# A 1x1 depthwise-separable convolution on one core: early loads dealt to two queues in another way, x's first chunk held by a semaphore, two filler matmul pairs and a warm-up copy dropped

## The chip, the core and the metric

The kernel runs on one core of a Trainium2 chip. The metric is the device time of one execution in microseconds (us). Three runs of the kernel before gave 573.46 us at the median. A profiled execution has a time of its own, and its trace covers a span from the first to the last instruction that is a little shorter. The engines are named as in the profile: PE is TensorE (PEld its weight loads), DVE VectorE, ACT ScalarE, POOL GpSimd, SP SyncE. ACTq and SPq are the instruction streams of ACT and SP where they issue DMAs; each of the two has a DMA queue of its own (q10 for ACT and q1 for SP in the profile), and both queues use the same 16 DMA engines.

## The reference

`x` is bf16 `[1, 384, 384, 384]`, that is 147456 rows of 384 channels; `dw` is `[1, 1, 384]`, one factor a channel; `pw` is `[384, 384]`.

```python
H = W = 384; C = 384; k = 1
x  = normal(1, H, W, C) * 0.05      # bf16
dw = normal(k, k, C) * 0.05         # bf16
pw = normal(C, C) * 0.05            # bf16

out = x * dw[0, 0]                  # k = 1: no padding, one tap
return einsum('bhwc,cd->bhwd', out, pw)
```

So the result is `x @ (diag(dw) @ pw)`, one matrix product with a scaled weight.

## The kernel before

The 147456 rows are worked on in 288 supertiles of 512 rows. SP loads rows of x into SBUF (three big buffers X0 to X2, in chunks of 1, 2, 4, 5, 6 or 10 supertiles; the first four chunks hold one supertile each). DVE transposes them in 32 by 32 blocks of 32-bit words into T (lines 404 and 406), in two halves a supertile; two T buffers alternate. PE multiplies: a supertile is 12 steps of 4 matmuls that run side by side in the four row quarters of the array (line 264), with the scaled weight `w_r` as the moving operand, into one of two PSUM buffers. ACT copies PSUM to bf16 in SBUF (line 475), and SP stores it. The loop over supertiles counts semaphores; the order on each engine is the order in which the program was written.

The change lies ahead of that loop, in the first microseconds, where the weight is made:

- Four loads are issued ahead of everything else (helper `load_early`, line 118): `dw` and the three 128-row parts of `pw` (k = 0, 1, 2, tile `raw`), and x's first chunk, 384 KB (tile `X`). The other loads of x follow on SP (line 170).
- PE fills the time with matmuls on constant ones, whose results nobody reads: two passes of four in `idle_work` ahead of the section, two more behind (line 134), two pairs at line 295 and some pairs between the useful ones.
- Three tiny matmuls turn dw into a column (line 282), DVE makes selection matrices scaled by dw from it (line 435), and for each k and r = 0, 1 a pair of matmuls (line 295) puts the scaled, regrouped rows of pw's part k into PSUM. These are called units i = 2k + r below. Each increments `s_w`.
- The units are copied from PSUM to `w_r` (line 422), by the table `w_units` of (unit, from, to, engine): unit 0 by ACT, unit 1 half by ACT and half by DVE, unit 2 by DVE, units 3, 4 and 5 by ACT, each engine in this order.
- Behind its two copies, DVE makes the first three transposes of x's first chunk (line 404); it comes to them only when its copies are done.
- PE starts the loop when units 0 to 3 are in `w_r` and the first transpose is done. Unit 4 is first needed at the ninth of the twelve steps, unit 5 at the eleventh.

On ACT a small copy to a tile `warm` (line 377) stands ahead of the `w_r` copies, and an activation table load ahead of that. The copy, and a memset on DVE, also give PSUM's two buffers free at the start (`s_a`).

Of the kernel before, what the change touches and what calls it, by code (L numbers as in the profile page):

```python
# [9 lines left out]
F32 = mybir.dt.float32  # L10
# [17 lines left out]
def kernel(  # L28
# [12 lines left out]
    nc = tc.nc  # L41
    P = nc.NUM_PARTITIONS
    B, H, W, C = x.shape
    assert dw.shape[0] == 1 and dw.shape[1] == 1, "only k=1 depthwise supported"
    D = pw.shape[1]
# [4 lines left out]
    xf = x.rearrange("b h w c -> (b h w) c")  # L50
# [25 lines left out]
    pw_n = raw[:, 0 : 3 * D].rearrange("p (k d) -> p k d", d=D)  # L76
# [6 lines left out]
    warm = consts.tile([P, 2], F32, name="warm")  # L83
# [3 lines left out]
    X0_h = nc.alloc_sbuf_tensor("X0", [P, 4 * LMAX, C], BF16)  # L87
# [5 lines left out]
    PS_h = [nc.alloc_psum_tensor(f"ps{s}", [P, 4, 512], F32) for s in range(2)]  # L93
    PS = [h.ap() for h in PS_h]

    s_x = [[nc.alloc_semaphore(f"s_x{i}{k}") for k in range(max(map(len, groups[i::NR])))] for i in range(NR)]
# [5 lines left out]
    s_a = [nc.alloc_semaphore(f"s_a{i}") for i in range(2)]  # L102
# [4 lines left out]
    s_pw = [nc.alloc_semaphore(f"s_pw{k}") for k in range(3)]  # L107
# [2 lines left out]
    s_dwf = nc.alloc_semaphore("s_dwf")  # L110
    s_sel = nc.alloc_semaphore("s_sel")
    s_w = nc.alloc_semaphore("s_w")
    s_wr = [nc.alloc_semaphore(f"s_wr{e}") for e in range(2)]

    early = []

    def load_early(eng, dst, src, sem):
        ins = eng.dma_start(dst, src).then_inc(sem, 16)  # L118
        tc.no_tile_sem_insts.add(ins.ins.name)
        early.append(ins.ins.name)  # L120

    dw_e = dataclasses.replace(dw_h, donated_from="early_dw").ap()
    pw_e = [dataclasses.replace(raw_h, donated_from=f"early_pw{k}").ap()[:, D * k : D * k + D] for k in range(3)]
    load_early(nc.scalar, dw_e, dw.rearrange("a e c -> a (e c)"), s_dw)
    for k in range(3):
        load_early(nc.scalar if k == 2 else nc.sync, pw_e[k], pw[P * k : P * k + P, :], s_pw[k])
    x0 = xf[0:512, :].rearrange("(p s) c -> p (s c)", p=P)
    X0_e = dataclasses.replace(X0_h, donated_from="early_x0").ap()[:, 0:4].rearrange("p s c -> p (s c)")
    load_early(nc.sync, X0_e, x0, s_x[0][0])

    def idle_work(ps, n):
        for _ in range(n):
            for i in range(4):
                mm = nc.tensor.matmul(  # L134
                    ps[:, 2 * (i % 2) + i // 2, :D],
                    lhsT=ones[32 * i : 32 * i + 32, 0:P],
                    rhs=ones[32 * i : 32 * i + 32, :],
                    start=True,
                    stop=True,
                    tile_position=(32 * i, 0),  # L140
                )
        return mm

    mm = idle_work(dataclasses.replace(PS_h[0], donated_from="early_ps").ap(), 2)
    early.append(mm.ins.name)

    with tc.tile_critical(sync_engine=mybir.EngineType.Pool, no_gpsimd_drain=True) as section:
        in_order = mybir.DependencyInfo(mybir.DependencyClass.NoSync, mybir.DependencyReason.SCHED_ONLY)
# [65 lines left out]
        def w_after(i):  # L214
            n = [sum(u[3] == e and u[0] <= i for u in w_units) for e in range(2)]
            return [(s_wr[e], n[e]) for e in range(2)]
# [64 lines left out]
        for k in range(3):  # L281
            mm = nc.tensor.matmul(  # L282
                PS[1][:, 2 + (k > 0), D + k : D + k + 1],
                lhsT=dw_row[:, P * k : P * k + P],
                rhs=ones[0:1, 0:1],
                start=True,
                stop=True,
            )
# [3 lines left out]
        def pair(out, lhsT, rhs, cols):  # L292
            for v in range(2):
                rows = slice(64 * v, 64 * v + 64)
                mm = nc.tensor.matmul(  # L295
                    out[:, v, :cols], lhsT=lhsT[rows], rhs=rhs[rows, :cols], start=True, stop=True, tile_position=(64 * v, 0)
                )
            return mm
# [3 lines left out]
        for k in range(3):  # L302
            for r in range(2):
                sel_kr = sel_w[:, k, r].rearrange("p q w -> p (q w)")
                if r == 0:
                    nc.tensor.wait_ge(s_pw[k], 16)
                if k == 0 or r == 0:
                    nc.tensor.wait_ge(s_sw, r + 1 if k == 0 else k + 2)
                if (k, r) == (0, 1):
                    nc.tensor.wait_ge(s_dwf, 2)  # L310
                if k == 2:
                    for sem, v in w_after(r):
                        if v:
                            nc.tensor.wait_ge(sem, v)

                if k == 2:
                    pair(PS[1][:, 2 * r :], sel_kr, pw_n[:, k, :], D if r == 0 else D // 2)
                pair(PS[(k + 1) % 2][:, 2 * r :], sel_kr, pw_n[:, k, :], D).then_inc(s_w)
                if (k, r) == (0, 1):
                    pair(PS[0], sel_kr, pw_n[:, k, :], D // 2)  # L320
# [22 lines left out]
        for m in range(4):  # L343
            if m == 1:
                nc.tensor.wait_ge(s_t[1][1], NS // 2)
            for par in range(2):
                mm = nc.tensor.matmul(  # L347
                    PS[1][:, m, :D],
                    lhsT=Tk[:, P * (m + 2) : P * (m + 3), par],
                    rhs=w_k[:, par, :],  # L350
                    start=False,
                    stop=par == 1,
                )
# [18 lines left out]
        for n in range(4):  # L372
            for g in range(4):
                x_b = Xl[quads[g], n, 256:384].rearrange("p (b c) -> p b c", c=64)
                nc.gpsimd.tensor_copy(Xk[quads[n], g:8:4, :], x_b).then_inc(s_xk)  # L375
                nc.gpsimd.tensor_copy(Xk[quads[n], 8 + g : 24 : 4, :], Xl[quads[g], :, 64 * n : 64 * n + 64]).then_inc(s_xk)  # L376
        nc.scalar.copy(warm[:, 0:1], nc.const_aps.tensor(0.0, [P, 1], F32)).then_inc(s_a[0])  # L377
        nc.vector.memset(warm[:, 1:2], 0.0).then_inc(s_a[1])

        def transposes(t, j):  # L380
            g, i, off, first, L = chunks[t]
# [61 lines left out]
        ins = nc.vector.tensor_copy(dw_f[:], dw_p[:, 1, 1:3])  # L443
# [10 lines left out]
        for jj, (t, j) in enumerate(order):  # L454
            g, i, off, first, L = chunks[t]
            s = jj % 2
# [64 lines left out]
```

## Time and profile before

| what | us |
|---|---|
| median of 3 runs | 573.46 |
| lowest and highest of them | 573.25, 575.51 |
| profiled execution, its own time | 573.07 |
| span of its trace | 571.1 |
| PE busy | 566.3 |
| DVE busy | 509.8 |
| ACT busy | 418.0 |
| first matmul of the loop starts at | 5.92 |

The page shows PE busy in nearly all of the span, and a DMA share of nine tenths or more in most of its slices at a mean of 397 GB/s. The loop's matmuls (line 264) have 559.8 us of PE's 566.3. What stands ahead of the loop is best read in the timeline of the first seven microseconds, beside the chain of work that ended last, whose first pieces are the early issues on SP and x's first chunk. A row of the timeline gives the start, the length, the engine, the line, the operation and the count; a bracket behind it gives the idle time before it and what ended it.

### The profile page before, as it was taken

Reading aid. Unit: us, or ns where it says so; the run is one execution under the profiler, and the core shown is the slowest. Engines: PE = TensorE matmul, PEld = TensorE weight load, DVE = VectorE, ACT = ScalarE, POOL = GpSimd, SP = SyncE. Lnnn points to the kernel's source line nnn. Section 1 sums busy time; section 2 is a strip of 40 time slices with the busy share of each in tenths; the row PEclk is TensorE's granted clock in tenths of the full one; section 3 lists DMA queues with packets and bytes.
Section 4 is the critical chain, followed back from the end, with each engine's and each line's share of the span. In section 5 each row is a group of like instructions: output and inputs, shape, how many; then the busy total and the mean of one; then the engine's idle time right before and its main releaser. Section 6 shows DMA issues by size and latency. Waiting matters only on the chain.

```text
span 571.1 us, 29717 instructions
## 1 busy us (share of the span) xinstructions
PE 566.3 (99%) x13841; PEld 359.1 (63%) x13841; DVE 509.8 (89%) x591; ACT 418.0 (73%) x297; POOL 13.9 (2%) x41
## 2 busy tenths in 40 slices
PE   8999999999999999999999999999999999999997
PEld 5666666666666666666666666666666666666664
DVE  7899999999999999999999999999999899998996
ACT  6777777777777777777777777777777777777775
POOL 2042000000000000000000000000000000000000
PEclk9999999999999999999999999999999999999999
DMA  8999999999999999999999999999999999998777
GB/s 325 436 406 391 431 418 426 436 427 410 430 433 431 404 388 425 405 383 398 431 386 396 410 427 386 409 400 421 402 394 431 402 387 402 420 394 322 312 286 269
DMA packets 28100, 226.88 MB, mean 397 GB/s; under 512 B 1465, under 2 KB 7866, under 8 KB 24122
## 3 DMA queue, kind: packets, MB, share of 16 engines
q1 hardware_dynamic: 27012, 225.81, 97.5%
q10 hardware_dynamic: 1078, 0.98, 0.5%
q14 instruction: 9, 0.07, 0.0%
q8 instruction: 1, 0.02, 0.0%
HBM read 113.54 MB, written 113.25 MB: 397 GB/s over the span
## 4 chain that ended last, share of the span: by engine, by line
PE 98%; DMA 1%; SPq 0%; ACT 0%; DVE 0%; issue 0%
PE ps L264 98%; DMA X<-in_x_dram 1%; PE ps L347 0%; SPq L118 0%; PE ps L335 0%; ACT O L470 0%; DVE T L404 0%
## 5 line engine op out<-in xcount | busy, mean ns | idle before, releaser
L264 PE MATMUL ps<-w_r,T 32*128 32x384 bf16 x13776 | 559.8, 321 | 0.6 <-DVE T L404 0.6
L406 DVE STREAM_TRANSPOSE T<-X 128x384 uint32<-128x384 uint32 x571 | 501.2, 879 | 53.5 <-DMA X<-in_x_dram 0.8
L475 ACT CAST O<-ps 128x1536 bf16<-128x1536 f32 x286 | 411.4, 1438 | 147.1 <-PE ps L264 147.1
L264 PEld LDWEIGHTS ps<-w_r,T 32*128 32x128 bf16 x13776 | 356.2, 93 | 204.2 <-DVE T L404 1.0
L376 POOL COPY Xk<-Xl 32x256 bf16<-32x256 bf16 x16 | 6.3, 394 | 0.0
L375 POOL COPY Xk<-Xl 32x128 bf16<-32x128 bf16 x16 | 4.6, 287 | 25.7 <-DMA Xl<-in_x_dram 24.9
L370 POOL COPY raw<-w_r 32x768 bf16<-32x768 bf16 x4 | 3.3, 819 | 5.7 <-ACT w_r L422 5.5
L422 ACT CAST w_r<-ps 128x768 bf16<-128x768 f32 (+1 forms) x5 | 3.3, 741 | 0.1
L377 ACT ACT_TABLE_LOAD x1 | 1.3, 1283 | 1.9 <-issue 1.9
L295 PE MATMUL ps<-raw 64*128 64x384 bf16 (+1 forms) x18 | 2.3, 419 | 0.0
L134 PE MATMUL ps<-const-bfloat16-1.0 32*128 32x384 bf16 x16 | 1.5, 515 | 0.8 <-PEq L505 0.8
L466 DVE CAST O<-ps 128x384 bf16<-128x384 f32 x2 | 1.0, 553 | 1.4 <-PE ps L264 1.4
L295 PEld LDWEIGHTS ps<-raw 64*128 64x128 bf16 x18 | 1.1, 116 | 1.5 <-DMA raw<-in_pw_dram 1.2
L406 DVE STREAM_TRANSPOSE T<-Xl 128x384 uint32<-128x384 uint32 x2 | 1.8, 884 | 0.2
L422 DVE CAST w_r<-ps 128x384 bf16<-128x384 f32 (+1 forms) x2 | 1.4, 758 | 0.2 <-PE ps L295 0.2
L389 DVE STREAM_TRANSPOSE T<-Xk 128x384 uint32<-128x384 uint32 x2 | 1.2, 578 | 0.5 <-PE ps L264 0.4
L347 PE MATMUL ps<-raw,T 128*128 128x384 bf16 x8 | 1.5, 328 | 0.0
L470 ACT CAST O<-ps 128x384 bf16<-128x384 f32 x2 | 1.0, 478 | 0.7 <-PE ps L347 0.7
L470 DVE CAST O<-ps 128x384 bf16<-128x384 f32 x2 | 1.1, 558 | 0.1
L465 ACT CAST O<-ps 128x384 bf16<-128x384 f32 x2 | 0.9, 482 | 0.5 <-PE ps L264 0.5
L347 PEld LDWEIGHTS ps<-raw,T 128*128 128x128 bf16 x8 | 0.7, 98 | 0.7 <-issue 0.3
L435 DVE TENSOR_SCALAR raw<-sel,ps 128x128 bf16<-128x128 f32 x2 | 0.5, 287 | 0.6 <-PE ps L282 0.6
(19 smaller groups left out, 5.8 us busy)
## 6 DMA issues: line engine op xcount, KB each, us to landing
X<-in_x_dram SPq DMA_DIRECT2D x25, 3840.0 KB, 21.8
out_dram<-O SPq DMA_DIRECT2D x25, 3840.0 KB, 27.8
X<-in_x_dram SPq DMA_DIRECT2D x3, 1536.0 KB, 18.0
X<-in_x_dram SPq DMA_DIRECT2D x2, 1920.0 KB, 15.6
out_dram<-O SPq DMA_DIRECT2D x2, 1920.0 KB, 24.4
out_dram<-O SPq DMA_DIRECT2D x2, 1536.0 KB, 12.9
X<-in_x_dram SPq DMA_DIRECT2D x6, 384.0 KB, 4.9
out_dram<-O SPq DMA_DIRECT2D x3, 768.0 KB, 5.3
```

Source lines behind the costliest of these rows:

```text
L134: mm = nc.tensor.matmul(ps[:, 2 * (i % 2) + i // 2, :D], lhsT=ones[32 * i : 32 * i + 32, 0:P], rhs=ones[32 * i : 32 * i + 32, :], start=Tr ...
L264: mm = nc.tensor.matmul(PS[s][:, q, :D], lhsT=Ts[s][32 * q : 32 * q + 32, b, par::2], rhs=w_r[32 * q : 32 * q + 32, b, par, :], start=(b, ...
L295: mm = nc.tensor.matmul(out[:, v, :cols], lhsT=lhsT[rows], rhs=rhs[rows, :cols], start=True, stop=True, tile_position=(64 * v, 0))
L347: mm = nc.tensor.matmul(PS[1][:, m, :D], lhsT=Tk[:, P * (m + 2) : P * (m + 3), par], rhs=w_k[:, par, :], start=False, stop=par == 1,)
L370: nc.gpsimd.tensor_copy(w_k[quads[n]], w_r[quads[n], n]).then_inc(s_wk)
L375: nc.gpsimd.tensor_copy(Xk[quads[n], g:8:4, :], x_b).then_inc(s_xk)
L376: nc.gpsimd.tensor_copy(Xk[quads[n], 8 + g : 24 : 4, :], Xl[quads[g], :, 64 * n : 64 * n + 64]).then_inc(s_xk)
L377: nc.scalar.copy(warm[:, 0:1], nc.const_aps.tensor(0.0, [P, 1], F32)).then_inc(s_a[0])
L406: ins = nc.vector.transpose(out=Tw[:, 3 * h : 3 * h + 3], in_=Xw[:, :, j, 96 * h : 96 * h + 96].rearrange("p k (b w) -> p b k w", w=32),)
L422: o = nc.vector.tensor_copy(out, in_) if e == 0 else nc.scalar.copy(out, in_)
L470: o = (nc.scalar.copy if n % 2 else nc.vector.tensor_copy)(Ov[:, n, j, :], PS[s][:, n, :D])
L475: a = nc.scalar.copy(Ov[:, :, j, :], PS[s][:, :, :D])
```

## The change

Four edits, all ahead of the loop:

1. pw's second part (k = 1) is loaded by ACT's queue, behind dw, where SP's queue had it; pw's third part (k = 2) stays on ACT's queue and so comes behind the second.
2. x's first chunk is now the second load on SP's queue, behind pw's first part, and waits for a new semaphore `s_e`. PE increments it with the last matmul of its first filler pass.
3. The two filler pairs ahead of units 4 and 5 on PE are left out.
4. The copy to `warm` on ACT is left out; DVE sets both halves of `warm` and both semaphores by two memsets.

```diff
-        load_early(nc.scalar if k == 2 else nc.sync, pw_e[k], pw[P * k : P * k + P, :], s_pw[k])
-    x0 = xf[0:512, :].rearrange("(p s) c -> p (s c)", p=P)
-    X0_e = dataclasses.replace(X0_h, donated_from="early_x0").ap()[:, 0:4].rearrange("p s c -> p (s c)")
-    load_early(nc.sync, X0_e, x0, s_x[0][0])
+        load_early(nc.scalar if k else nc.sync, pw_e[k], pw[P * k : P * k + P, :], s_pw[k])
...
-    mm = idle_work(dataclasses.replace(PS_h[0], donated_from="early_ps").ap(), 2)
-    early.append(mm.ins.name)
+    ps_e = dataclasses.replace(PS_h[0], donated_from="early_ps").ap()
+    for i in range(2):
+        mm = idle_work(ps_e, 1)
+        if i == 0:
+            mm.then_inc(s_e)
+            tc.no_tile_sem_insts.add(mm.ins.name)
+        early.append(mm.ins.name)
+
+    x0 = xf[0:512, :].rearrange("(p s) c -> p (s c)", p=P)
+    X0_e = dataclasses.replace(X0_h, donated_from="early_x0").ap()[:, 0:4].rearrange("p s c -> p (s c)")
+    load_early(nc.sync, X0_e, x0, s_x[0][0])._wait_ge(s_e, 1)
...
-                if k == 2:
-                    pair(PS[1][:, 2 * r :], sel_kr, pw_n[:, k, :], D if r == 0 else D // 2)
                 pair(PS[(k + 1) % 2][:, 2 * r :], sel_kr, pw_n[:, k, :], D).then_inc(s_w)
...
-        nc.scalar.copy(warm[:, 0:1], nc.const_aps.tensor(0.0, [P, 1], F32)).then_inc(s_a[0])
-        nc.vector.memset(warm[:, 1:2], 0.0).then_inc(s_a[1])
+        for i in range(2):
+            nc.vector.memset(warm[:, i : i + 1], 0.0).then_inc(s_a[i])
```

Lines move by a few: 118 becomes 119, 134 becomes 133, 264 becomes 272, 295 becomes 303, 404 becomes 410, 422 becomes 428.

On SP, from the program's start, the kernel before has these rows (`raw` is pw's tile, `X` x's first buffer; the counts behind a row are equal instructions in sequence):

```order
L516 UNCONDITIONAL_BRANCH [waits barrier_Pool_Activation_PE_DVE_SP_release]
L118 DMA raw<-in_pw_dram 128x384 x2
L118 DMA X<-in_x_dram 128x1536
L516 UNCONDITIONAL_BRANCH [waits Pool_sequencer_49]
L170 DMA X<-in_x_dram 128x1536 x3
```

and the changed kernel, at the same place on SP:

```order
L522 UNCONDITIONAL_BRANCH [waits barrier_Pool_Activation_PE_DVE_SP_release]
L119 DMA raw<-in_pw_dram 128x384
L119 DMA X<-in_x_dram 128x1536 [waits s_e]
L522 UNCONDITIONAL_BRANCH [waits Pool_sequencer_49]
L178 DMA X<-in_x_dram 128x1536 x3
```

One load of pw is gone from ahead of x's first chunk, which has got a wait; all later loads of x stand behind that wait.

On ACT, from the program's start to the `w_r` copies, before:

```order
L118 DMA dw_row<-in_dw_dram 1x384
L118 DMA raw<-in_pw_dram 128x384
L516 UNCONDITIONAL_BRANCH [waits Pool_sequencer_49]
L377 ACT_TABLE_LOAD
L377 COPY warm<-const-float32-0.0 128x1
L422 CAST w_r<-ps 128x2x384 [waits s_w]
```

and changed:

```order
L119 DMA dw_row<-in_dw_dram 1x384
L119 DMA raw<-in_pw_dram 128x384 x2
L522 UNCONDITIONAL_BRANCH [waits Pool_sequencer_49]
L428 ACT_TABLE_LOAD
L428 CAST w_r<-ps 128x2x384 [waits s_w]
```

A third DMA issue stands ahead of the table load, and the copy behind it is gone; the table load still comes ahead of the first wait for `s_w`.

On PE, from unit 2 to the loop (`raw` here holds pw's parts and the scaled selection matrices), before:

```order
L295 MATMUL ps<-raw 128x384 [waits s_sw,s_pw1]
L295 MATMUL ps<-raw 128x384 x3
L295 MATMUL ps<-raw 128x384 [waits s_wr1,s_sw,s_pw2]
L295 MATMUL ps<-raw 128x384 x3
L295 MATMUL ps<-raw 128x192 [waits s_wr1,s_wr0]
L295 MATMUL ps<-raw 128x192
L295 MATMUL ps<-raw 128x384 x2
L321 UNCONDITIONAL_BRANCH
```

and changed:

```order
L303 MATMUL ps<-raw 128x384 [waits s_sw,s_pw1]
L303 MATMUL ps<-raw 128x384 x3
L303 MATMUL ps<-raw 128x384 [waits s_wr1,s_sw,s_pw2]
L303 MATMUL ps<-raw 128x384
L303 MATMUL ps<-raw 128x384 [waits s_wr1,s_wr0]
L303 MATMUL ps<-raw 128x384
L327 UNCONDITIONAL_BRANCH
```

Two filler matmuls of 384 columns and two of 192 are gone; units 4 and 5 still stand behind the wait for pw's third part, and ahead of the loop.

More of the change, by code (lines that the diff above doesn't have):

```diff
@@ L112 @@
     s_w = nc.alloc_semaphore("s_w")
+    s_e = nc.alloc_semaphore("s_e")
     s_wr = [nc.alloc_semaphore(f"s_wr{e}") for e in range(2)]
@@ L120, in load_early @@
         early.append(ins.ins.name)
+        return ins
     dw_e = dataclasses.replace(dw_h, donated_from="early_dw").ap()
```

## The prediction

> **What bounds the kernel now.** I read the page first (busy times and groups), then the stretch from 20 to 560 us, then the chain of work that ended last, then the first seven microseconds row by row. From the page, the groups of instructions (count, busy us, mean ns, idle time before them), and then the row of the stretch 20 to 560 us:
>
> ```profile
> L264 PE MATMUL ps<-w_r,T 32*128 32x384 bf16 x13776 | 559.8, 321 | 0.6 <-DVE T L404 0.6
> L406 DVE STREAM_TRANSPOSE T<-X 128x384 uint32<-128x384 uint32 x571 | 501.2, 879 | 53.5 <-DMA X<-in_x_dram 0.8
> ```
> ```profile
> core 0: us, PE busy (x) PEld busy (x) DVE busy (x) ACT busy (x) POOL busy (x), PEclk, DMA share, GB/s
> 20.00:560.00 540.00, 540.00 (x13300) 343.76 (x13296) 487.90 (x555) 398.31 (x278) 10.09 (x32) 1.00 0.99 402
> ```
>
> PE is busy for all 540 of 540 us, and the loop's matmuls lost only 0.6 us in all, to DVE's first transposes at line 404. No edit touches the loop, so its 559.8 us stay. What can change is when it starts. The chain of work (start, us, what), over the first 20 us:
>
> ```profile
> 0.80 0.39 SPq L118
> 1.20 0.06 issue
> 1.26 0.41 SPq L118
> 1.67 0.05 issue
> 1.72 3.82 DMA X<-in_x_dram
> 5.53 0.02 issue
> 5.55 0.32 DVE T L404
> 5.88 0.05 issue
> 5.92 14.14 PE ps L264 x341
> ```
>
> Two pw issues, then x's first chunk issued at 1.72 and landed 3.82 later, at 5.53-5.54; 0.32 for the first transpose, and the loop starts at 5.92. The weights run beside it (timeline of ACT and DVE):
>
> ```profile
> 1.93 1.28 ACT L377 ACT_TABLE_LOAD   x1 [1.93 <-issue]
> 3.22 0.19 ACT L377 COPY warm<-const-float32-0.0 128x1 f32<-128x1 f32 x1
> 3.48 3.32 ACT L422 CAST w_r<-ps 128x768 bf16<-128x768 f32 x5
> ...
> 3.80 1.44 DVE L422 CAST w_r<-ps 128x384 bf16<-128x384 f32 x2 [0.22 <-PE ps L295]
> 5.55 0.70 DVE L404 STREAM_TRANSPOSE T<-X 128x128 uint32<-128x128 uint32 x3 [0.32 <-DMA X<-in_x_dram]
> ```
>
> DVE has finished its weight copies at 3.80 + 1.44 = 5.24 and waits 0.32 us for x. So the x path has no more than about 0.3 us to give before DVE's own weight copies hold the loop. That is the ceiling of the gain: 0.05% of the time.
>
> **The change, part by part.** 0.5% of this kernel is 2.9 us, about what its measurement can tell from no change; every term below is far smaller.
>
> *x's first chunk.* The hold is PE's first filler pass, and the issue behind pw's first part is bounded by this row and by the next issue slot on SP:
>
> ```profile
> 0.84 0.51 PE L134 MATMUL ps<-const-bfloat16-1.0 32*128 32x384 bf16 x4 [0.84 <-PEq L505]
> ```
>
> The pass ends at 1.35; with the 0.05 us that the chain shows from a signal to its taker, SP issues at 1.40, against 1.72. Without the hold it could have gone at 1.26, where the second pw load stood, so the hold costs 0.14 of the 0.46 that the freed slot gives. Bounds of the gain in issue time: 0.2 (a slower wake-up) to 0.46. With the same 3.82 us to land: 5.22. Behind the waiting instruction on SP stand only the other loads of x, which then also go 0.3 us sooner.
>
> *pw's second part.* It moves from SP at 1.26 to ACT behind dw, at 1.37, where pw's third part stood. How long such loads take to land (KB each, median us):
>
> ```profile
> raw<-in_pw_dram SPq DMA_DIRECT2D x2, 96.0 KB, 2.1
> raw<-in_pw_dram ACTq DMA_DIRECT2D x1, 96.0 KB, 2.9
> ```
>
> Two ends: 1.37 + 2.1 = 3.47 and 1.37 + 2.9 = 4.27; before it was 1.26 + 2.1 = 3.4. I take 4.27, because the ACT row is the same queue, the same issue time and a load that ran beside x's first chunk, and x now comes earlier still. The stretches 3.20 to 4.00 show the collision (all DMAs: last column GB/s), and the packets of the ACT queue q10 in 2.6 to 2.8, its first ones of pw, and then in 3.2 to 3.4, 3.6 to 3.8 and 3.8 to 4.0 (none in between):
>
> ```profile
> 3.20:3.40 0.20, 0.20 (x4) 0.15 (x2) 0.20 (x2) 0.19 (x2) 0.00 (x0) 1.00 2.25 211
> 3.40:3.60 0.20, 0.20 (x6) 0.05 (x2) 0.18 (x1) 0.13 (x2) 0.00 (x0) 1.00 0.17 15
> 3.60:3.80 0.20, 0.20 (x6) 0.19 (x4) 0.00 (x0) 0.20 (x1) 0.00 (x0) 1.00 0.34 69
> 3.80:4.00 0.20, 0.20 (x4) 0.07 (x2) 0.20 (x1) 0.20 (x1) 0.00 (x0) 1.00 0.63 253
> ```
> ```profile
> q10 hardware_dynamic: 17, 0.01, 24.2%
> ...
> q10 hardware_dynamic: 11, 0.01, 9.0%
> ...
> q10 hardware_dynamic: 2, 0.00, 2.2%
> ...
> q10 hardware_dynamic: 6, 0.00, 6.8%
> ```
>
> When x's first packets start, nearly nothing moves for some 0.4 us (15 and 69 GB/s), and ACT's last 8 packets of pw come only afterwards. In the kernel before only these stragglers of the third part were caught. Now x's packets should start about 0.3 us sooner, at the time when ACT's queue starts its first pw load, so the second part as a whole meets that standstill.
>
> What follows from 4.27: PE takes unit 2 at 4.32. The matmul rows of 3.9 to 4.2 and DVE's copy of unit 2:
>
> ```profile
> L295 PE MATMUL ps<-raw 64*128 64x384 bf16 x4 | 0.8, 524 | 0.0
> ...
> 4.28 0.96 DVE L422 CAST w_r<-ps 128x768 bf16<-128x768 f32 x1
> ```
>
> 4.32 + 0.52 + 0.03 = 4.87; DVE's copy ends at 4.87 + 0.96 = 5.83 instead of 5.24, and x, landed at 5.22, now waits for DVE. First transpose and hand-over, 0.32 + 0.05: the loop starts at 6.20, 0.28 later than before. By the other end, 3.47, PE is ready for unit 2 no sooner than before, DVE ends at 5.24, and the loop starts at 5.24 + 0.37 = 5.61, 0.31 sooner. The two meet where pw's second part lands at 5.55 - 0.96 - 0.55 - 0.05 = 3.99.
>
> [...]
>
> *pw's third part.* Issued at 1.37 + 0.37 + 0.05 = 1.79. Ends: 1.79 + 2.9 = 4.69, or 1.79 + 3.82 = 5.61 if it fares as x's chunk does. Units 4 and 5 stand ahead of the loop on PE, two pairs of 0.16 us at the loop's pace or 0.32 at the slow one (rows under D). At 4.69 they are through by 5.4, far ahead of 6.20; at 5.61 by about 6.0 to 6.3, still nearly covered by DVE. I take 0; the high end adds 0.2 if the loop otherwise would start early.
>
> *ACT.* The rows of the issue that there is now one more of, and of unit 3's copy:
>
> ```profile
> 1.37 0.37 ACTq L118 DMA_DIRECT2D raw<-in_pw_dram  x1
> ...
> 4.60 0.80 ACT L422 CAST w_r<-ps 128x768 bf16<-128x768 f32 x1
> ```
>
> One issue more, 0.37 + 0.03, moves the table load from 1.93 to 2.33; it ends at 3.61, and the first weight copy starts at 3.62 instead of 3.48. The dropped copy of 0.19 gives part of it back already. Unit 3, needed at the loop's start, would by that end at 5.40 + 0.14 = 5.54, just ahead of the earliest start worked out above. ACT's five copies were back to back (3.48 + 3.32 = 6.80), so the last would end at 6.94 and, if unit 3 comes 0.3 later too, at about 7.1. Unit 5 is needed ten steps of 0.163 us (559.8 / 3444) into the loop, at 7.55 or later. Covered, with 0.4 to spare. If that cover went, each 0.1 us would be a 0.1 us stall, once.
>
> *Fillers and memset.* The dropped pairs took PE 0.16 + 0.08 us (fast) to 0.32 + 0.16 (slow), ahead of ACT copies that stood back to back anyway: no gain. The second memset goes where DVE waits for POOL:
>
> ```profile
> 1.47 0.29 DVE L427 TENSOR_REDUCE sel<-eye 128x64 f32<-128x128 bf16 x1 [0.33 <-POOL eye L357]
> ```
>
>  A loss is possible through PE's speed, below.
>
> *Sum:* 573.07 + 0.28 = 573.35 for the profiled execution, which lies 0.39 below the median of the runs; against that median, 573.7.
>
> **The rivals.**
>
> *pw in time (B).* Unit 2's load lands by 3.99 or sooner: loop start 5.61, or 0.31 sooner, 573.15. For it speaks that only some 8 of the third part's 128 rows were still to come behind the standstill; against it, that x now starts sooner.
>
> *Nothing moves (C).* The standstill, not the issue time, sets when x lands; or gain and loss cancel. Start 5.92, 573.5.
>
> *PE stays slow (D), the one that ends slower.* Two filler passes in one row, and then the mean of one 384-column matmul at 1.4 to 1.7, at 4.95 to 5.2, and in the loop at 6.4 to 6.6:
>
> ```profile
> 0.84 0.83 PE L134 MATMUL ps<-const-bfloat16-1.0 32*128 32x384 bf16 x8 [0.84 <-PEq L505]
> ...
> L134 PE MATMUL ps<-const-bfloat16-1.0 32*128 32x384 bf16 x8 | 0.9, 523 | 0.0
> ...
> L295 PE MATMUL ps<-raw 64*128 64x384 bf16 x4 | 0.6, 323 | 0.0
> ...
> L264 PE MATMUL ps<-w_r,T 32*128 32x384 bf16 x16 | 0.8, 321 | 0.0
> ```
>
> PE starts slow (the second pass adds 0.32 us to the first one's 0.51, against 0.163 a step in the loop) and is fast some 3.8 us after its first matmul, though the clock column says 1.00 throughout. The change takes work from PE just ahead of that point: it would wait from 3.7 to 4.3 for pw, and the pairs are gone. If PE had to earn its speed anew in the loop, 3.8 us at half speed cost 1.9 us: 575.4 (+0.33%). It passes the 0.5% only if the slow stretch in the loop is longer than 5.7 us. [...]
>
> **How the numbers follow.** Forecast A (pw late, start near 6.2): 0.45. B: 0.25. C: 0.13. D: 0.15. Something outside these: 0.02. The predicted time is A's, 573.7. A, B and C lie between 572.9 and 574.2; the range reaches from 572.7 into D, to 575.0, and leaves out D's upper half and little below. All of A, B and C are within 0.5%, and most of D; slower by over 0.5% is D's tail and half of the unknown, 0.05; faster needs 2.9 us from a start of 5.92, which must hold the 3.8 us of x's load, so 0.02.
>
> **What would show it.** Right: the chain's head is PE line 303 and DVE line 428 instead of x's load, x lands near 5.2 with DVE still at line 428, PE waits 0.3 to 0.6 us for pw ahead of unit 2, the loop starts at 6.1 to 6.3. B: DVE at line 410 starts by 5.3. C: x lands at 5.5. D: line 272 has rows of 500 ns behind 6 us. Wrong altogether: waits of PE in the stretch from 20 to 560 us, or a change of over 2.9 us with the loop's start near 6.

## The result

The changed kernel takes 576.17 us at the median (8 runs, 575.15 to 577.88), the kernel before 573.40 (8 runs, 572.79 to 575.51): the ratio is 1.0041 (95% interval 1.0023 to 1.0058). It is slower by 0.4%, and 1.2 us above the upper end of the forecast's range. The profiled execution of the changed kernel is its shortest one, 575.15 us with a span of 573.2 (before: 573.07 and 571.1).

Behind its start, the loop is still without a stall. From the page, the loop's matmuls, and the row of the stretch 20 to 560 us:

```profile
L272 PE MATMUL ps<-w_r,T 32*128 32x384 bf16 x13776 | 560.8, 321 | 0.1
```
```profile
20.00:560.00 540.00, 540.00 (x13300) 370.97 (x13292) 486.31 (x554) 398.28 (x277) 10.09 (x32) 1.00 0.99 401
```

PE is again busy for 540 of 540 us there. The loop's own busy time has grown by 1.0 us (559.8 before), and it starts later. The chain of work that ended last, over the first 20 us:

```profile
1.37 0.39 ACTq L119
1.76 0.03 issue
1.79 4.32 DMA raw<-in_pw_dram
6.11 0.05 issue
6.16 0.82 PE ps L303 x4
6.98 0.07 issue
7.05 13.00 PE ps L272 x289
```

x's first chunk is gone from the chain. In its place stands pw's third part, issued on ACT's queue at 1.79 and landed at 6.11 (4.30 before), with units 4 and 5 on PE behind it. The loop starts at 7.05 instead of 5.92: 1.13 us later. The second part is just as late (timeline of SP, PE, DVE and ACT; the bracket gives the idle time and what ended it):

```profile
1.39 0.34 SPq L119 DMA_DIRECT2D X<-in_x_dram  x1
...
5.24 1.74 PE L303 MATMUL ps<-raw 64*128 64x384 bf16 x8 [1.27 <-DMA raw<-in_pw_dram]
5.79 0.96 DVE L428 CAST w_r<-ps 128x768 bf16<-128x768 f32 x1 [1.37 <-PE ps L303]
6.10 2.20 ACT L428 CAST w_r<-ps 128x768 bf16<-128x768 f32 x3 [1.21 <-PE ps L303]
6.66 0.69 DVE L410 STREAM_TRANSPOSE T<-X 128x128 uint32<-128x128 uint32 x3
```

It landed at 5.20 (3.37 before), and PE, DVE and ACT all stood idle for 1.2 to 1.4 us for it. x's first chunk was issued at 1.39, landed at 4.99 by its last semaphore step, and then lay ready: its transposes start at 6.66, behind DVE's weight copy.

The second half of the loss is PE's speed. Mean ns of one of the loop's matmuls at 7 to 7.5, 8 to 8.5 and 9.5 to 10 us:

```profile
L272 PE MATMUL ps<-w_r,T 32*128 32x384 bf16 x8 | 0.8, 506 | 0.1
...
L272 PE MATMUL ps<-w_r,T 32*128 32x384 bf16 x12 | 1.2, 520 | 0.0
...
L272 PE MATMUL ps<-w_r,T 32*128 32x384 bf16 x20 | 1.0, 321 | 0.0
```

PE was at half speed until 9.08, the time at which the trace's first record of a full clock stands (4.68 in the kernel before, where no matmul of the loop was slow): 28 of the loop's matmuls lie in the 2.03 us from 7.05 to 9.08, 56 in the next 2.03. Half speed from 7.05 to 9.08 costs half of 2.03 us, 1.0. Together 1.13 + 1.0 = 2.1 us, the difference of the two spans, 573.2 - 571.1. The medians lie 2.77 us apart. The other 0.7 us are in executions of which there is no trace; what makes them is not shown.

### The profile page after: what moved, and what is told of

Read it like the earlier page. It is cut to its first block, busy times and chain, and to the rows that moved or that the text cites. A ratio compares the mean times of both kernels' runs of the same rounds, so it can differ in the third digit from the quotient of the medians.

```text
span 573.2 us, 29709 instructions
## 1 busy us (share of the span) xinstructions
PE 567.6 (99%) x13837; PEld 387.5 (68%) x13837; DVE 508.8 (89%) x592; ACT 417.8 (73%) x296; POOL 13.9 (2%) x41
## 4 chain that ended last, share of the span: by engine, by line
PE 98%; DMA 1%; ACTq 0%; ACT 0%; issue 0%
PE ps L272 98%; DMA raw<-in_pw_dram 1%; PE ps L353 0%; ACTq L119 0%; PE ps L303 0%; PE ps L341 0%; ACT O L476 0%
## 5 line engine op out<-in xcount | busy, mean ns | idle before, releaser
L272 PE MATMUL ps<-w_r,T 32*128 32x384 bf16 x13776 | 560.8, 321 | 0.1
L272 PEld LDWEIGHTS ps<-w_r,T 32*128 32x128 bf16 x13776 | 384.8, 93 | 176.3 <-DVE T L410 0.7
```

What stands on the lines that cost most here:

```text
L272: mm = nc.tensor.matmul(PS[s][:, q, :D], lhsT=Ts[s][32 * q : 32 * q + 32, b, par::2], rhs=w_r[32 * q : 32 * q + 32, b, par, :], start=(b, ...
```

## The experiments

All but e11 and e12 start from the changed kernel. Theory 1 was that the order of the loads does it all: x's first chunk keeps pw's second part from the DMA engines, PE idles, and the idling delays its full speed. Against it stood the dropped fillers, the dropped warm-up copy, and a slow ACT queue. What the trace of each kernel shows, in us from the span's start; the last two columns compare two terms alone, the later start and half of the loop's slow stretch, with the measured span:

| kernel | pw 2nd part | pw 3rd | x first | loop starts | loop slow | start + half of slow | span - 571.1 |
|---|---|---|---|---|---|---|---|
| before | 3.37 | 4.30 | 5.53 | 5.92 | - | 0 | 0 |
| changed | 5.20 | 6.11 | 4.99 | 7.05 | to 9.08 | 2.1 | 2.1 |
| e1 | 3.42 | 3.62 | 5.46 | 5.85 | - | -0.1 | -0.1 |
| e2 | 5.86 | 6.51 | 5.66 | 7.52 | to 10.54 | 3.1 | 3.0 |
| e3 | 5.57 | 6.15 | 5.38 | 7.42 | - | 1.5 | 1.5 |
| e4 | 4.49 | 5.79 | 5.50 | 6.59 | to 8.90 | 1.8 | 1.8 |
| e5 | 3.63 | 3.88 | 6.49 | 6.88 | 7.12 to 10.53 | 2.7 | 2.6 |
| e6 | 4.21 | 5.48 | 5.20 | 6.28 | to 9.93 | 2.2 | 2.1 |
| e7 | 3.38 | 5.05 | 5.55 | 5.94 | - | 0.0 | 0.3 |
| e8 | 5.24 | 6.53 | 5.07 | 7.33 | to 9.05 | 2.3 | 2.2 |
| e9 | 4.39 | 6.43 | 4.09 | 7.00 | 7.62 to 11.03 | 2.8 | 2.7 |
| e10 | 5.46 | 5.64 | 5.29 | 7.31 | to 10.01 | 2.7 | 2.7 |
| e11 | 4.09 | 4.27 | 5.71 | 6.28 | - | 0.4 | 0.3 |
| e12 | 3.46 | 3.75 | 5.46 | 5.86 | to 7.66 | 0.8 | 0.8 |

In e7 x's first chunk is two loads, and 5.55 is the landing of both. Two terms are enough for every kernel to within 0.1 us, but for e7. There SP issues x's later chunks at 2.91 instead of 2.35 in the kernel before, DVE waits 0.69 and 0.72 us for the second and the third of them, and PE's matmuls start 0.31 and 0.26 us apart at 7.75 and 9.87, where 0.16 is usual: that is most of the 0.3 us.

**e1: pw's second part back on SP's queue**

```diff
-        load_early(nc.scalar if k else nc.sync, pw_e[k], ...)
+        load_early(nc.scalar if k == 2 else nc.sync, pw_e[k], ...)
```

> The changed kernel with pw's second part back on SP's queue, ahead of x's first chunk (whose wait for the first filler pass is then long met); the filler pairs and the warm copy stay out. Theory 1 (the order of the loads does it all: x's first chunk holds up pw's second part on ACT's queue, PE idles for it, and the idling delays PE's full speed): pw's second part lands near 3.4, the loop starts at 5.6 to 6.0, PE is at full speed by about 5 us, ratio to the kernel before 0.999 to 1.001. Theory 2 (the dropped filler pairs delay PE's full speed): loop start near 5.9 but matmuls of 500 ns in its first microseconds, ratio 1.002 to 1.003. Theory 3 (the dropped warm copy delays ACT's weight copies): loop start 6.2 or later.

Measured: 573.25 us against 573.30, ratio 1.0005 (0.9993 to 1.0017). The chain's end, and the loop's matmuls at 6 to 7 us:

```profile
4.10 1.42 DVE w_r L428 x2
5.53 0.27 DVE T L410
5.80 0.05 issue
5.84 8.29 PE ps L272 x197
...
L272 PE MATMUL ps<-w_r,T 32*128 32x384 bf16 x30 | 1.5, 322 | 0.4 <-DVE T L410 0.4
```

The loop starts at 5.84-5.85 and its matmuls are fast from the first. So the whole loss goes with one word in the order of the loads, and the dropped fillers and the dropped copy cost nothing that shows within the interval, as theory 1 has it; theories 2 and 3 fall. The word changes two things: pw's second part is back on SP's queue, and x's first chunk goes behind it, as late as in the kernel before. e4, e5 and e8 take the two apart.

**e2: the filler pairs put back**

```diff
+                if k == 2:
+                    pair(PS[1][:, 2 * r :], sel_kr, pw_n[:, k, :], D if r == 0 else D // 2)
                 pair(PS[(k + 1) % 2][:, 2 * r :], sel_kr, pw_n[:, k, :], D).then_inc(s_w)
```

> The changed kernel with its two filler pairs ahead of units 4 and 5 put back. Theory 1: pw's second part still lands at 5.0 to 5.3, the loop starts near 7.1, and PE gets its full speed as late as in the changed kernel; ratio 1.003 to 1.006. Theory 2: full speed by about 5 to 6 us, loop start near 7.1, ratio 1.002.

Measured: 575.81, ratio 1.0041 (1.0025 to 1.0056), the changed kernel's own. The second part landed at 5.86, later than the 5.0 to 5.3 expected. This trace holds records of PE's speed going both ways; the stretches 5 to 7, 7 to 9, 9 to 11 and 11 to 13 (PEclk is the third column from the right):

```profile
5.00:7.00 2.00, 0.94 (x12) 0.42 (x12) 0.71 (x1) 0.55 (x1) 0.00 (x0) 1.00 1.03 396
7.00:9.00 2.00, 1.82 (x26) 0.78 (x24) 2.00 (x7) 1.65 (x3) 0.20 (x1) 0.53 1.06 438
9.00:11.00 2.00, 2.00 (x36) 1.05 (x32) 1.10 (x2) 0.00 (x0) 1.88 (x3) 0.61 1.04 439
11.00:13.00 2.00, 2.00 (x56) 1.23 (x52) 1.75 (x2) 1.44 (x1) 1.20 (x2) 1.00 1.05 441
```

Full from 3.72, half from 7.13, full from 10.54 by the clock records: PE had got its speed and lost it again after it idled for pw.

**e3: PE kept busy while it waits**

```diff
+                if r == 0 and k:
+                    if k == 2:
+                        for sem, v in w_after(0):
+                            if v:
+                                nc.tensor.wait_ge(sem, v)
+                    for _ in range(4 if k == 1 else 1):
+                        pair(PS[k - 1], ones[:, 0:P], ones, D)
                 if r == 0:
                     nc.tensor.wait_ge(s_pw[k], 16)
```

> The changed kernel with filler matmuls where PE waits: four pairs ahead of unit 2 and one ahead of unit 4, so that PE has work while pw's second and third parts come. Theory 1, with the idle time as the cause of the late full speed: loop start still 6.8 to 7.2, but its matmuls at 320 ns from the start; 1.0 us or more is won back of what the change lost, ratio 1.001 to 1.003. If the idle time is not the cause of the late speed: 500 ns matmuls to about 9 us as in the changed kernel, ratio 1.004 or more.

Measured: 574.69, ratio 1.0025 (1.0014 to 1.0035). The loop starts at 7.42, later than in the changed kernel, and yet (matmuls at 7.5 to 8):

```profile
L272 PE MATMUL ps<-w_r,T 32*128 32x384 bf16 x16 | 0.8, 322 | 0.5 <-DVE T L417 0.5
```

Its matmuls are fast from the start, and 1.5 of the 2.8 us between the medians of the changed kernel and of the kernel before are won back. What is left, 574.69 - 573.30 = 1.4 us, is the later start (1.5). So the two halves of the loss come apart, and PE's idling makes the second; e12 shows the same from the other side.

**e4: x held to the second filler pass**

```diff
-        if i == 0:
+        if i == 1:
             mm.then_inc(s_e)
```

> The changed kernel with x's first chunk held to the second filler pass, so that it is issued at about 1.7, as in the kernel before, and pw's second part has a lead of 0.3 us. Theory 1 (a collision in time): most of pw's second part passes ahead of x, lands at 3.4 to 4.3, the third at 4.5 to 5.2, x at 5.4 to 5.6; loop start 5.9 to 6.4, ratio 1.000 to 1.002. Rival (ACT's queue is slow for pw whenever x is on the other queue, whatever the lead): pw's second part lands after 5, ratio 1.004.

Measured: 574.77, ratio 1.0016 (1.0002 to 1.0029). x goes at 1.71, as before the change, and pw's second part lands at 4.49, the third at 5.79; both later than expected (3.4 to 4.3 and 4.5 to 5.2), and the loop starts at 6.59. The packets of ACT's queue at 2.4 to 2.8 and 2.8 to 3.2 us:

```profile
q10 hardware_dynamic: 96, 0.07, 69.8%
...
q10 hardware_dynamic: 31, 0.02, 41.1%
```

These are 96 and 31, against none and one in the changed kernel (rows under e7), and 12 of the second part's 16 semaphore steps had come by 3.27: a lead of 0.3 us lets most of it through ahead of x. The other four steps come between 3.95 and 4.49; that x was first on their DMA engines is likely, but the trace does not name a packet's engine. The lead counts, then, and the rival of an ACT queue that is slow beside x in any case falls.

**e5: x held until pw's second part has landed**

```diff
-    load_early(nc.sync, X0_e, x0, s_x[0][0])._wait_ge(s_e, 1)
+    load_early(nc.sync, X0_e, x0, s_x[0][0])._wait_ge(s_pw[1], 16)
```

> The changed kernel with x's first chunk held until pw's second part has landed, so that nothing of x is in flight while ACT's queue loads pw's second part. Theory 1 (x's packets keep pw's second part from the DMA engines): the part lands at 3.2 to 3.6, issued at the same 1.37 as in the changed kernel. x is issued at about 3.5 and lands at 6.6 to 7.3, which then sets the loop's start at 7.0 to 7.7: ratio 1.002 to 1.006. Rival (ACT's queue behind dw is slow by itself): the part lands at 4.5 or later.

Measured: 575.54, ratio 1.0034 (1.0023 to 1.0044). The chain:

```profile
1.37 2.25 DMA raw<-in_pw_dram
3.63 0.02 issue
3.64 2.85 DMA X<-in_x_dram
```

Issued at the same 1.37 on the same queue, the part lands after 2.25 us with x away, where it took 3.83 with x. The third lands right behind, at 3.88. ACT's queue is not slow by itself: x's chunk makes the second part late. x then sets the start (6.88), and PE, which had waited 1.52 us, lost its speed at 7.12.

**e6: x on ACT's queue, pw on SP's**

```diff
-        load_early(nc.scalar if k else nc.sync, pw_e[k], ...)
+        load_early(nc.sync, pw_e[k], ...)
...
-    load_early(nc.sync, X0_e, x0, s_x[0][0])._wait_ge(s_e, 1)
+    load_early(nc.scalar, X0_e, x0, s_x[0][0])._wait_ge(s_e, 1)
```

> The changed kernel with the queues exchanged: pw's three parts on SP's queue, x's first chunk (still held to the first filler pass) on ACT's queue behind dw. If it is x's large packets that win wherever they stand: pw's second part lands at 4.2 or later though it is on SP's queue, x at about 5.0. If ACT's queue loses against SP's whatever they carry: pw's second part at 3.4 to 3.8 and the third by 4.3, x's first chunk at 5.5 or later and the loop starts with it.

Measured: 575.02, ratio 1.0018 (1.0003 to 1.0032). pw's second part lands at 4.21 and the third at 5.48 though they are on SP's queue, x at 5.20. So pw is late beside x on SP's queue too: the third part, issued at 1.72 behind x (1.39), lands 0.3 us behind it. The second part, issued at 1.26 ahead of x, lands 1.0 us ahead of it and is not as late as on ACT's queue. Its lead is longer here (0.13 us, where the changed kernel has 0.02), so the run does not say whether the queue matters beside the lead.

**e7: x in rows of pw's size**

```diff
-    x0 = xf[0:512, :].rearrange("(p s) c -> p (s c)", p=P)
-    X0_e = ....ap()[:, 0:4].rearrange("p s c -> p (s c)")
-    load_early(nc.sync, X0_e, x0, s_x[0][0])._wait_ge(s_e, 1)
+    for b in range(2):
+        x0 = xf[0:512, :].rearrange("(p a b) c -> b p a c", p=P, b=2)[b]
+        X0_e = ....ap()[:, b:4:2]
+        load_early(nc.sync, X0_e, x0, s_x[0][0])._wait_ge(s_e, 1)
```

> The changed kernel with x's first chunk loaded by two DMAs of 768-byte rows in place of one of 3072-byte rows, both behind the same hold. If the DMA engines take turns packet by packet, so that x's packets of four times pw's size take most of the time: pw's second part lands 0.5 us or more sooner than in the changed kernel, at 3.8 to 4.6. If it is the standstill at the start of x, or the order in which descriptors come: 5.0 or later as in the changed kernel.

The wait for x's first chunk counts both loads. Measured: 574.24, ratio 1.0018 (1.0008 to 1.0027); the profiled execution is the shortest of the ten, 573.36. The part landed at 3.38, sooner than either theory said. The packets of the two queues at 2.4 to 2.8 and 2.8 to 3.2 us, first here and then in the changed kernel (q1 is SP's queue, q10 ACT's):

```profile
q10 hardware_dynamic: 91, 0.07, 65.7%
q1 hardware_dynamic: 7, 0.00, 2.2%
...
q1 hardware_dynamic: 18, 0.01, 54.5%
q10 hardware_dynamic: 49, 0.03, 22.0%
```
```profile
q1 hardware_dynamic: 18, 0.05, 72.0%
...
q1 hardware_dynamic: 25, 0.08, 64.2%
q10 hardware_dynamic: 1, 0.00, 10.7%
```

The hold is the same and x's issue starts at the same 1.39, but its packets come some 0.4 us later in this form, and so pw's second part went first (91 packets of ACT's queue to 7 of SP's at 2.4 to 2.8); the third came late beside x, at 5.05. x itself landed no sooner than in the kernel before (5.55 against 5.53). The run does not tell of the packets' size, then, since it changed who was first as well; that this is what counts fits it, and is shown by e4 and e5.

**e8: no hold**

```diff
-    load_early(nc.sync, X0_e, x0, s_x[0][0])._wait_ge(s_e, 1)
+    load_early(nc.sync, X0_e, x0, s_x[0][0])
```

> The changed kernel without the hold: x's first chunk is issued at 1.26, ahead of pw's second part (1.37). Theory 1: pw's second part is at least as late as in the changed kernel, 5.2 to 5.9, x lands at 4.8 to 5.2, loop start 7.0 to 7.6, ratio 1.004 to 1.006: the hold of 0.13 us does little for or against.

Measured: 576.65, ratio 1.0067 (1.0050 to 1.0084). The second part lands at 5.24, the third at 6.53. The hold to the first filler pass came 0.13 us behind the free slot, too little to let pw through.

**e9: half of x's first chunk**

```diff
-    x0 = xf[0:512, :].rearrange("(p s) c -> p (s c)", p=P)
-    X0_e = ....ap()[:, 0:4].rearrange("p s c -> p (s c)")
+    x0 = xf[0:512, :].rearrange("(p s) c -> p (s c)", p=P)[:, 0 : 2 * C]
+    X0_e = ....ap()[:, 0:2].rearrange("p s c -> p (s c)")
...
+        nc.vector.memset(Xs[0][:, 2:4].rearrange('p s c -> p (s c)'), 0.0)
```

> The changed kernel with only half of x's first chunk loaded (1536 bytes a row in place of 3072; a memset on DVE stands for the other half, so the first supertile is computed from half of its data). Theory 1a (a DMA engine finishes its whole share of x's chunk, 8 rows, before it turns to ACT's queue): the share is half as long, pw's second part lands 0.4 us or more sooner than the 5.2 to 5.9 of the changed kernel and its near copies. Theory 1b (x's queue goes ahead as long as it has anything, the next chunk too): no sooner than 5.1.

The half that is not loaded is zeros here, so half of the first 512 rows of the result are not computed from x. Measured: 574.96, ratio 1.0023 (1.0013 to 1.0033). PE's waits for the second and the third part, and the landing of the halved chunk (issued at 1.39; KB, us):

```profile
4.43 0.50 PE L303 MATMUL ps<-raw 64*128 64x384 bf16 x4 [0.51 <-DMA raw<-in_pw_dram]
6.47 0.50 PE L303 MATMUL ps<-raw 64*128 64x384 bf16 x4 [1.54 <-DMA raw<-in_pw_dram]
```
```profile
X<-in_x_dram SPq DMA_DIRECT2D x1, 192.0 KB, 2.7
```

x lands at 4.09 and pw's second part at 4.39, 0.8 us sooner than in the changed kernel, while x's next, whole chunk stood behind in the same queue, with packets from 3.66 on. So pw need not wait for x's whole queue, and 1b falls. The packets of the changed kernel at 3.2 to 3.6 and 3.6 to 4.0 us fit 1a:

```profile
q1 hardware_dynamic: 38, 0.12, 75.5%
q10 hardware_dynamic: 7, 0.01, 8.4%
...
q10 hardware_dynamic: 72, 0.06, 40.7%
q1 hardware_dynamic: 38, 0.09, 54.7%
```

ACT's queue moves next to nothing until 3.6, and 72 packets in the next 0.4 us, as x's first chunk runs out: its first semaphore steps come from 4.06 on. That an engine turns to ACT's queue just when it has done its whole share of x is not shown, since no packet's engine is named; what is measured is that only 8 packets of ACT's queue start from 2.4 to 3.6, and that the part lands 0.2 us behind x. The third part comes amid the next, whole chunk of x (6.62): 6.43.

**e10: x's later chunks held**

```diff
+        nc.sync.wait_ge(s_pw[2], 16)
         for _, f, a in sorted(todo, key=lambda a: a[0]):
```

> The changed kernel with x's second and later chunks held until pw's third part has landed. Theory 1a: pw's second part still has to wait for x's first chunk and lands at 4.2 to 4.8, the third right behind it, by 5.0 (6.1 in the changed kernel); loop start 6.2 to 6.6, x's second chunk lands after 7.5 and may stall DVE once. Theory 1b: pw's second part lands at about 4.2 too, so the two are told apart by the run with half a chunk. If later chunks of x play no part: 5.2 and 6.1 as in the changed kernel.

Measured: 575.78, ratio 1.0044 (1.0028 to 1.0060). The rows of the issues (KB each, us to landing; x was issued at 1.40):

```profile
X<-in_x_dram SPq DMA_DIRECT2D x1, 384.0 KB, 3.9
raw<-in_pw_dram ACTq DMA_DIRECT2D x2, 96.0 KB, 4.0
```

The numbers expected for the second part, 4.2 to 4.8, and for the loop's start, 6.2 to 6.6, were missed; behind x's chunk, which landed at 5.29, they could not have come true. The second part came at 5.46, as late as if x's later chunks played no part, and the third at 5.64. The order is 1a's: each comes 0.2 us behind the one before, and with no second chunk of x in the way the third part lands 0.5 us sooner than in the changed kernel. The loop starts no sooner for it (7.31): that is 1.85 us behind the second part, as in the changed kernel (5.20 and 7.05).

**e11: the kernel before with more fillers**

```diff
+        for sem, v in w_after(2):
+            nc.tensor.wait_ge(sem, v)
+        for _ in range(2):
+            pair(PS[0], ones[:, 0:P], ones, D)
         with nc.tensor.Fori(0, NS // 2 - 1, 1) as it:
```

> The kernel before with two more filler pairs on PE, behind unit 5, where PE waits for x's first chunk. If idle time of PE in the first microseconds is what makes some executions of the kernel before 2 us longer than the others: fewer of them are, the rest are unchanged at about 573.2; ratio 0.998 to 1.000. If not: 1.000, with one in ten at 575 as before.

Measured: 573.60 against 573.41, ratio 1.0003 (0.9994 to 1.0012): no gain. In the trace PE is at the fillers until the loop starts, at 6.28, 0.4 us later than in the kernel before. No execution of either kernel reached 574.1 in this comparison, so it cannot say whether the fillers would spare the longer ones. None of these kernels beats the kernel before.

**e12: the kernel before with fewer fillers**

```diff
-        idle_work(PS[0], 2)
+        idle_work(PS[0], 1)
...
-        for _ in range(2):
-            pair(PS[0], ones[:, 0:P], ones, D)
...
-                if k == 2:
-                    pair(PS[1][:, 2 * r :], sel_kr, pw_n[:, k, :], D if r == 0 else D // 2)
...
-                if (k, r) == (0, 1):
-                    pair(PS[0], sel_kr, pw_n[:, k, :], D // 2)
```

> The kernel before without any filler behind the first three passes: no pairs ahead of unit 0, none behind unit 1, none ahead of units 4 and 5; the loads stay as they were. If PE's idle time by itself delays its full speed, whatever the loads do: loop start 5.8 to 6.0 as before, but in most executions matmuls of 500 ns in the loop, 1 to 2 us more, ratio 1.001 to 1.004. If only the late loads count: 1.000.

Measured: 574.99, ratio 1.0024 (1.0013 to 1.0034). Loop matmuls at 6 to 7 and 8 to 8.5 us, and the chain's last step:

```profile
L264 PE MATMUL ps<-w_r,T 32*128 32x384 bf16 x16 | 1.5, 516 | 0.4 <-DVE T L398 0.4
...
L264 PE MATMUL ps<-w_r,T 32*128 32x384 bf16 x20 | 1.0, 321 | 0.0
```
```profile
5.85 14.20 PE ps L264 x321
```

The loads are those of the kernel before and the loop starts at 5.85, as early as ever; only PE had less to do until then. It is slow to 7.66, where the kernel before has full speed from 4.68. PE's idle time alone delays its speed, without any late load. The trace has 0.8 us of the 1.6 between the medians; the rest is in executions without a trace.

## Why the prediction was wrong

Right: the loop untouched; x's issue (1.40 forecast, 1.39) and landing (5.22 forecast, 4.99); the chain's head moved from x's chunk to pw on ACT's queue, with DVE's copy of unit 2 between x and its transposes, which is the mechanism of forecast A; copy, memset and fillers at nothing (e1), and the later table load too, since ACT waits 1.21 us for PE behind its first copies in the changed kernel.

Three steps failed.

- *"I take 4.27"* for pw's second part was too early by 0.9 us, and this is the step that set the loss going: it landed at 5.20, and in e2, e3 and e8 at 5.86, 5.57 and 5.24. The ACT row's 2.9 us was the wrong neighbour, since in the kernel before 15 of the third part's 16 semaphore steps had come by 3.61 and the last one alone made it 4.30. Without a lead to speak of (0.02 us at the issue in the changed kernel, against 0.3 in e4), the part lands shortly behind x itself: 0.2 us behind it in the changed kernel, in e2, e3, e8 and e10, 0.3 in e9. The bound to take was x's own landing, 5.2 by the forecast's own sum, not the row of a load that had mostly slipped past. With 5.20 in place of 4.27 that sum gives a start of 7.13; 7.05 was measured, so the rest of the path was right. The standstill at 3.4 to 3.8 was misread as well: the view counts a packet's bytes and time where the packet starts, hence the DMA share of 2.25 just ahead of it. By the packets' own times, 11 packets of x and nothing else are in flight there from 3.4 to 3.6, and the first ones of x take up to 1.0 us each. So x's packets were under way in that stretch; how many of the engines they held is not shown.
- *"I take 0"* for the third part, with a landing at 5.61 as the high end: it landed at 6.11, a further chunk of x behind the second. The landing was wrong, and the 0 held here by luck: units 4 and 5 end at 6.98, when DVE's path behind the second part (copy of unit 2 to 6.75, first transpose to 6.97) ends as well, and in e10 an earlier third part won nothing. In e4, e6 and e8 the third part does set the start, 0.8 us behind its landing.
- *A and D were given as rivals, and they are one mechanism.* The wait for pw that makes A is the idle time that makes D. With the wait of 1.27 us, D came with it in the profiled execution (1.13 and 1.0 us), and the loop's 559.8 us, which were to stay, became 560.8. The other seven executions have no trace; all of them took longer. D's own price, up to 1.9, was an upper end: 1.0 here, 1.7 in e5 and e9. The sum A + D, 573.46 + 0.28 + 1.9 = 575.6, was never made, and the range ended at 575.0.

## What to carry to other kernels

A small load on one queue, needed by the next step, can land behind the whole of a large one on another: pw's 96 KB took 3.83 us beside x's 384 KB and landed 0.2 us behind them, and took 2.25 us with x away (e5). Here it came down to whose packets were first: a lead of 0.3 us at the issue (e4) let most of the small load through. Price such a load by the landing of the large one it meets, not by its own time in a trace where it had the engines to itself. And where PE starts slow (520 ns a matmul here, 321 later), a stall ahead of the loop may have to be counted twice, once as a later start and once as slow matmuls behind it (1.13 and 1.0 us here). Forecasts that rest on the same wait are not rivals: add their prices.

## What had not been expected of the hardware

- PE's speed changed at steps of 3.41 us in the three traces that record more than one change early on (3.72, 7.13, 10.54 in e2; 3.71, 7.12, 10.53 in e5; 4.20, 7.62, 11.03 in e9), and full speed was refused or taken back behind stretches of that length in which PE had been idle for a part of the time only. The rows below give such a stretch's ends, its length and PE's busy time in it, for e12 and e4 (the one behind which PE stayed slow, then the one that ends with full speed) and e7 (full speed at its end). The stretches ahead of a first record are counted back by 3.41; that the steps go on there is the author's estimate from the three traces:

```profile
0.84:4.25 3.41, 2.54 (x23) 0.90 (x23) 1.81 (x8) 2.09 (x3) 0.29 (x1) 1.00 0.62 170
4.25:7.66 3.41, 3.02 (x31) 1.20 (x32) 3.26 (x8) 2.68 (x5) 0.59 (x1) 1.00 1.02 360
```
```profile
2.08:5.49 3.41, 2.67 (x21) 0.81 (x17) 2.14 (x7) 2.55 (x4) 0.00 (x0) 1.00 0.88 260
5.49:8.90 3.41, 3.07 (x36) 1.41 (x40) 2.69 (x8) 2.21 (x3) 0.82 (x2) 1.00 1.04 410
```
```profile
2.37:5.78 3.41, 2.88 (x18) 0.97 (x18) 2.81 (x8) 3.31 (x5) 0.00 (x0) 1.00 0.85 213
```

  Behind 2.67 of 3.41 us (78%, e4) PE stayed slow; behind 2.88 (84%, e7) it was fast, as behind 2.87 in e5. In e5 and e9, full speed was withdrawn behind stretches with 1.40 and 1.63 us (41% and 48%). In the changed kernel the stretch that ends at 5.67 had 2.14 us (63%), and PE stayed slow. The other kernels agree: slow behind 1.23 (e2), 1.82 (e10), 2.22 (e8) and 2.62 us (e6), fast behind 2.88 (e2) to 3.41 (before). That the share of such a stretch is what counts is read from these rows; it was not tried by itself.
- Where the changes fall differs from trace to trace. PE's first matmul stands at 0.84 in the traces of the kernel before, the changed kernel and e12, and the first record of full speed comes at 3.71 in e5 and at 6.34 in e3, where PE was kept busy. If the reading above holds, one and the same stall can cost nothing or most of 3.41 us at half speed, by where it falls: an estimate, not tried. That may be why executions of one kernel lie some 2 us apart (e4: 573.09 to 575.51); with one trace a kernel it is not shown.
- The clock column shows 1.00 ahead of a trace's first clock record (the rows of e12 above), where matmul durations of 500 ns and more (516 in e12, 506 to 520 in the changed kernel, against 321 later) say half speed. Durations are the reading to trust there.
- Many of the first packets of x's first chunk take 0.3 us and more each (9 of the first 32 in the changed kernel, up to 0.48; 14 of them in the kernel before, up to 1.03), where later ones of the same size take 0.12. Why that is was not tried.
